# Scores of the short last query tile: one unit at a time in two 64x64 tiles, or two units together in four

## The chip, the core and the metric

The kernel runs on one core of one Trainium2 chip. The metric is the device time of one execution in microseconds (us), smaller is better. A core has five engines with a queue each, worked off in order: TensorE (PE in the profile; PEld is its weight load), VectorE (DVE), ScalarE (ACT), GpSimd (POOL) and SyncE (SP, which here only issues DMAs). A number such as L303 is a line of the kernel before; all lines named here and in the prediction are lines of that file unless the text says otherwise.

## What is computed

Attention with a top-32 mask over 8 batches and 8 heads, 576 positions, head dimension 64, followed by a SwiGLU feed-forward block on the 4608 x 512 result, all in fp32:

```
scores = q @ k.T / 8                        # per batch and head: 576 x 576
kth    = 32nd largest of each row
attn   = softmax(scores where scores >= kth, else -1e9)
x      = (attn @ v), heads side by side     # 4608 x 512
out    = (silu(x @ w_gate) * (x @ w_val)) @ w_out     # d_ff 1536
```

## The kernel before

**Units.** The attention is cut into 160 units `(b, qt, hp)`: batch, query tile, pair of heads, with the pair innermost. 576 queries make four tiles of 128 and a rest of R = 64, so of the 20 units of a batch the first 16 are full (`qt` 0 to 3: 128 queries, two heads one after the other, each on all 128 partitions) and the last four are short (`qt == J`: 64 queries, the two heads of the pair above each other on the partitions). Positions inside a batch are called 0 to 19 below; 16 to 19 are the short ones. Units 16 and 17, and 18 and 19, are neighbours that `values` treats as a pair.

**A unit's way.** `scores` multiplies q by k on PE into PSUM banks of 288 columns and ACT copies these, scaled, into `sc` in SBUF. `select` finds the 32 largest of each row on DVE: four MAX8 and three MATCH_REPLACE8 per 128 rows (L337, L341). `shift` is a small POOL operation (L352). `weigh` makes the masked exponentials on ACT (Prelu L364, Exp L369). `normalize` divides by the sum (DVE L382, L383; ACT L387; POOL L389). `turn` transposes the weights on PE (L402) and ACT copies them out (L403). `values` multiplies two units' weights by v (PE L435) and ACT copies the result into `xT` (L451).

**The short unit's scores.** L303: for each of two halves of the keys a bank, and in it one matmul per head. Head 0 reads partitions 0 to 63 and writes partitions 0 to 63, head 1 reads and writes 64 to 127. So two of the four 64x64 quarters of the array are used, those on the diagonal. L308 copies the two banks out. The full unit (L317, L322) has two heads by two halves of the keys, four matmuls of 64 rows by 128 columns into four banks.

**PSUM.** `ps_t` has five banks with one tag, which the scores, the values and all transposes share; a new tile takes the bank that was free first.

**The order of work** is written out by hand in a loop over n; the last lines of the kernel pin every engine's instructions to the order in which the loop emits them. One turn n of the loop emits, in this order: what waits in `on_act`; `shift(n - 1)`; the first scores of `nxt`, matmuls and copies; at even n `values` of the two units n - 4 and n - 3; the matmuls of the second scores of `nxt`; `weigh(n - 1)` on ACT; the copies of the second scores on ACT; then, between the steps of `select(n)` on DVE, up to two pieces of feed-forward work, `turn(n - 2)`, key and query transposes of unit n + 3 (`fetch`), `normalize(n - 1)`, and more pieces. `scored(n)` says which scores a turn has: at even n those of n + 1 and n + 2, at odd n none.

**Feed-forward pieces.** `piece()` emits the next part of the feed-forward block (L579 for the first products, L645 for the second), each with a cost. How many are emitted in turn n is set by a credit: `share(n)` grants 6.4 (5.8 in the first 32 turns; half of it for a short unit) less an estimate of the other PE work in that turn, in which scores of a full unit count 0.7 and those of a short one 0.35. All pieces are done once, whatever the credit says; it moves them only between turns. From unit 156 on the credit is 8.

Of the kernel before, what the change touches and what calls it, by code (L numbers as in the profile page):

```python
# [8 lines left out]
AF = mybir.ActivationFunctionType  # L9
# [16 lines left out]
def kernel(  # L26
# [260 lines left out]
    def scores(n):  # L287
        b, qt, hp = units[n]
        slab = preps[b * NHP + hp]
        sc = work.tile([P, 2 * S], FP32, tag="sc", name="sc", bufs=3)  # L290
        halves = [slice(0, D), slice(D, P)]
        half = S // 2

        def bank():
            return ps_t.tile([P, 512], FP32, tag="t", name="s")


        if qt == J:
            banks = [bank() for _ in range(2)]
            for i, ps in enumerate(banks):  # L300
                for d in halves:
                    k0 = R + i * half
                    nc.tensor.matmul(  # L303
                        ps[d, 0:half], slab[d, S + R : S + 2 * R], slab[d, k0 : k0 + half]
                    )
            yield
            for i, ps in enumerate(banks):
                nc.scalar.mul(sc[:, i * half : (i + 1) * half], ps[:, 0:half], scale)  # L308
        else:
            q0 = S + 2 * R + qt * P  # L310
            banks = []
            for i in range(2):
                for hh, d in enumerate(halves):
                    ps = bank()
                    banks.append((i + 2 * hh, ps))
                    k0 = (1 - hh) * R + i * half
                    nc.tensor.matmul(  # L317
                        ps[:, 0:half], slab[d, q0 : q0 + P], slab[d, k0 : k0 + half]
                    )
            yield  # L320
            for i, ps in banks:
                nc.scalar.mul(sc[:, i * half : (i + 1) * half], ps[:, 0:half], scale)  # L322
        state[n] = dict(sc=sc)

    def select(n):

        nh = n_heads(units[n][1])
        sc = state[n]["sc"]
        m = small.tile([P, 2, TOP_K], FP32, tag="m", name="m")
        heads = [slice(t * S, (t + 1) * S) for t in range(nh)]  # L330
        e = work.tile([P, 2 * S], FP32, tag="e", name="e", bufs=3)
        state[n] |= dict(m=m, e=e, heads=heads)
        cur = sc
        rounds = TOP_K // 8
        for r in range(rounds):
            for t, hs in enumerate(heads):
                nc.vector.max(m[:, t, 8 * r : 8 * r + 8], cur[:, hs])  # L337
                yield
            if r < rounds - 1:
                for t, hs in enumerate(heads):  # L340
                    nc.vector.match_replace(  # L341
                        e[:, hs], m[:, t, 8 * r : 8 * r + 8], cur[:, hs], LOWEST
                    )
                    yield
                cur = e

    def shift(n):

# [8 lines left out]
    def weigh(n):  # L357


        st = state[n]  # L360
        sc, m, e, heads, bias = st.pop("sc"), st.pop("m"), st["e"], st["heads"], st.pop("bias")
        tot = small.tile([P, 2], FP32, tag="tot", name="tot")
        for t, hs in enumerate(heads):
            nc.scalar.activation(  # L364
                e[:, hs], sc[:, hs], AF.Prelu, bias=m[:, t, TOP_K - 1 : TOP_K], scale=-1.0,
                alpha=SMALL,
            )
        for t, hs in enumerate(heads):
            nc.scalar.activation(  # L369
                e[:, hs], e[:, hs], AF.Exp, bias=bias[:, t : t + 1], scale=-1.0 / SMALL,  # L370
                accum_out=tot[:, t : t + 1],
            )
        if n < AHEAD:
            nc.scalar.add(tot[:, 0 : len(heads)], tot[:, 0 : len(heads)], EPS)
        st["tot"] = tot
# [37 lines left out]
    def values(ns):  # L413

        b, qt, hp0 = units[ns[0]]
        last = qt == J
        ql = R if last else P
        av = ps_t.tile([P, 2, P], FP32, tag="t", name="av")
        for i, n in enumerate(ns):
            assert units[n] == (b, qt, hp0 + i)  # L420
            vt, v_last, vl = vs[b * NHP + hp0 + i]
            et = state.pop(n)["et"]
            for c in (*range(J), J) if last else (J, *range(J)):
                for hh in range(2):
                    d = slice(hh * R, (hh + 1) * R)
                    if c == J:
                        weights_, at = (v_last[:, hh, :], d) if last else (vl[:, d], None)
                    else:
                        weights_, at = vt[:, hh, c, :], d if last else None
                    moving = (  # L430
                        et[:, c, at]
                        if last
                        else et[:, c + (0 if c == J else hh * (J + 1)), :]
                    )
                    nc.tensor.matmul(  # L435
                        av[d, i, 0:ql],
                        weights_,
                        moving,
                        start=c == (0 if last else J),
                        stop=c == (J if last else J - 1),  # L440
                    )
        c0 = b * S + qt * P
        at = c0
        hps = slice(hp0, hp0 + len(ns))
        while at < c0 + ql:
            kb = at // BLK
            n_c = min((kb + 1) * BLK, c0 + ql) - at
            if kb not in xT:
                xT[kb] = ffn.tile([P, NHP, BLK], FP32, tag="xT", name="xT", bufs=3)
                done[kb] = 0  # L450
            nc.scalar.copy(  # L451
                xT[kb][:, hps, at - kb * BLK : at - kb * BLK + n_c],
                av[:, 0 : len(ns), at - c0 : at - c0 + n_c],
            )
            done[kb] += n_c * len(ns)
            at += n_c
# [331 lines left out]
    def share(n):  # L788


        others = 0.0
        costs = [(m, 0.7) for m in scored(n) + valued(n)] + [(n - TURN, 0.6)]
        for m, cost in costs:
            if m >= 0:
                others += cost * (0.5 if units[m][1] == J else 1)
        if units[n + 3][1] == 0:
            others += 0.6

        beside = 5.8 if n < AHEAD else 6.4
        return beside * n_heads(units[n][1]) / 2 - others  # L800

    def scored(n):

        ahead = [n + 1] if n < 2 else [] if n % 2 else [n + 1, n + 2]
        return [m for m in ahead if m < NU]

    def valued(n):

        behind = [] if n % 2 else [n - 4, n - 3]
        return [m for m in behind if 0 <= m < NU]  # L810
# [33 lines left out]
    for n in range(NU + 3):  # L844
        nh = n_heads(units[n][1]) if n < NU else 1
        topk = select(n) if n < NU else no
        norm = normalize(n - 1) if 0 <= n - 1 < NU else no
        nxt = [scores(m) for m in scored(n)]
        ahead = fetch(n + 3 if n else 2) if n + 3 < NU else no

        def dve(k, beside=True):

            for _ in range(k * nh):
                next(topk, None)
                due[0] += 5 / 6 if beside else 0
                if due[0] >= 1:
                    due[0] -= 1
                    rounding(1)

        if n >= NU - NHP:  # L860
            credit[0] = 8.0
        else:
            credit[0] = min(credit[0] + share(n), share(n) + 1)
        flush(on_act)
        if 0 <= n - 1 < NU:
            shift(n - 1)
        flush(on_pool)
        if nxt:
            run(nxt.pop(0))
        if valued(n):  # L870
            finish_units(valued(n))
        if nxt:
            next(nxt[0])
        early[0]()
        if 0 <= n - 1 < NU:
            weigh(n - 1)
        if nxt:
            run(nxt.pop())


        dve(2, beside=False)
        if n == 0:
            run(ahead)
            load(3)
            ahead = fetch(3)
        if n < NHP:
            load_v(n)
        pieces(2)
        flush(on_act)
        dve(1)  # L890
        dve(1)
        if 0 <= n - TURN < NU:
            run(turn(n - TURN))

        flush(on_pool)
        next(ahead, None)
        pieces(1)
        next(ahead, None)
        dve(1)
        pieces(1)  # L900
        if n < AHEAD:
            dve(1, beside=False)
        run(norm)
        dve(1 if n < AHEAD else 2, beside=False)
        run(topk)
        pieces(6)
# [50 lines left out]
```

## Time and profile before

| | |
|---|---|
| median of three runs | 1753.39 us (1752.44 to 1754.14) |
| the profiled execution | 1752.52 us, of which the span is 1750.7 us |
| PE busy | 1673.1 us, 96% of the span |
| DVE busy | 1475.4 us, 84% |
| ACT busy | 1262.1 us, 72% |
| POOL busy | 799.2 us, 46% |
| granted TensorE clock | 0.975 in the mean, below full in the first slices |
| the short units' score matmuls (L303) | 38.0 us |
| the full units' score matmuls (L317) | 173.0 us |

The span runs from the first to the last instruction; the execution has 1.8 us around it. A matmul of fp32 stands in the records twice (two passes), so a short unit's four matmuls are eight records. "Busy" is the time in which at least one record of a group is open, so matmuls that run beside each other count once; the mean is that of one record and is longer than its share of the time, since records overlap. The last unit's sums are inverted on DVE at 1682 us; after that PE works off the rest of the feed-forward block. An idle time is put down to the last thing that the waiting instruction needed.

### The profile page before, as it was taken

To read this page: it belongs to the slowest core of one execution; us is meant where nothing else is said; L and a number is where in the kernel's file an instruction comes from. 1 tells how busy PE (TensorE), PEld (TensorE's weight loads), DVE (VectorE), ACT (ScalarE), POOL (GpSimd) and SP (SyncE) were. 2 spreads that over 40 slices of the span, in tenths; PEclk is the share of its full clock that TensorE was granted. 3 is DMA by queue.
4 is the path that set the end of the run, shared out by engine and by line. 5 is a ranking of instruction groups with operands and counts; after the bars stand their busy time and mean duration, and the time that the engine had idled before them with its cause. 6 is when DMAs were issued, how large, how long until landed. Compare 5 with 4: busy or idle time off the path is not lost.

```text
span 1750.7 us, 31758 instructions
## 1 busy us (share of the span) xinstructions
PE 1673.1 (96%) x11408; PEld 1401.1 (80%) x11408; DVE 1475.4 (84%) x3311; ACT 1262.1 (72%) x2901; POOL 799.2 (46%) x914
## 2 busy tenths in 40 slices
PE   5679999999999999999999999999999999999999
PEld 3468688788888788887888878887888878788887
DVE  6999899989989899898999898898988988898300
ACT  7899787777767786768777777777776777676531
POOL 4799534343353425352535334443444433535334
PEclk6698999999999999999999999999999999999999
DMA  7442120003000120002100030000300020000000
GB/s 203 137 121 86 29 69 1 13 2 83 15 13 1 28 70 1 13 13 58 28 13 1 14 70 27 1 13 19 80 1 13 1 57 15 13 1 13 1 13 12
DMA packets 109309, 59.72 MB, mean 34 GB/s; under 512 B 88544, under 2 KB 96992, under 8 KB 109152
## 3 DMA queue, kind: packets, MB, share of 16 engines
q1 hardware_dynamic: 108016, 57.37, 12.6%
q8 instruction: 90, 1.47, 0.4%
q14 instruction: 67, 0.55, 0.1%
q10 hardware_dynamic: 1136, 0.33, 0.1%
HBM read 48.23 MB, written 9.44 MB: 33 GB/s over the span
## 4 chain that ended last, share of the span: by engine, by line
PE 79%; DVE 10%; ACT 6%; POOL 2%; issue 1%; SPq 1%; DMA 0%; POOLq 0%; ACTq 0%; DVEq 0%
PE f L579 36%; PE x_ps L645 9%; PE av L435 9%; PE s L317 7%; PE y_ps L645 6%; PE etps L402 6%; DVE m L337 5%; DVE e L341 4%; PE f L495 3%; ACT e L369 2%; PE s L303 2%; PE kqps L270 1%; DVE size L123 1%; PE o_ps L547 1%; ACT e L364 1%
## 5 line engine op out<-in xcount | busy, mean ns | idle before, releaser
L337 DVE MAX8 m<-e 128x8 f32<-128x576 f32 x864 | 614.8, 747 | 3.1
L341 DVE MATCH_REPLACE8 e<-m,e 128x576 f32<-128x576 f32 x576 | 423.8, 742 | 0.0
L579 PE MATMUL f<-xT,wg 128*128 128x256 f32 x1536 | 354.1, 381 | 0.0
L579 PE MATMUL f<-xT,wv 128*128 128x256 f32 x1536 | 353.9, 380 | 0.0
L579 PEld LDWEIGHTS f<-xT,wg 128*128 128x128 f32 x1536 | 287.0, 190 | 45.4 <-issue 8.4
L579 PEld LDWEIGHTS f<-xT,wv 128*128 128x128 f32 x1536 | 286.8, 190 | 42.7 <-issue 5.5
L615 POOL TENSOR_TENSOR h<-h,half_g 128x512 f32<-128x512 f32 x96 | 122.5, 1276 | 347.5 <-ACT h L614 331.6
L369 ACT ACTIVATE e<-e,bias 128x576 f32<-128x576 f32 x288 | 221.5, 778 | 34.6 <-POOL bias L352 31.3
L402 PE MATMUL etps<-ident,e 128*128 128x128 f32 x1312 | 183.3, 282 | 47.8 <-POOL e L389 20.8
L402 PEld LDWEIGHTS etps<-ident,e 128*128 128x128 f32 x1312 | 155.1, 144 | 78.3 <-POOL e L389 26.5
L364 ACT ACTIVATE e<-sc,m 128x576 f32<-128x576 f32 x288 | 212.1, 790 | 0.0
L341 DVE MATCH_REPLACE8 e<-m,sc 128x576 f32<-128x576 f32 x288 | 211.8, 742 | 0.0
L337 DVE MAX8 m<-sc 128x8 f32<-128x576 f32 x288 | 203.2, 742 | 7.3 <-ACT sc L322 7.3
L322 ACT ACTIVATE sc<-s 128x288 f32<-128x288 f32 x512 | 167.9, 418 | 53.8 <-PE s L317 53.4
L620 POOL TENSOR_TENSOR h<-h,val 128x512 f32<-128x512 f32 x96 | 122.4, 1275 | 175.1 <-ACT val L619 158.3
L389 POOL TENSOR_TENSOR e<-e,tot 128x576 f32<-128x576 f32 x140 | 160.7, 1152 | 89.3 <-DVE tot L383 76.0
L403 ACT COPY et<-etps 128x512 f32<-128x512 f32 (+1 forms) x448 | 184.2, 491 | 12.0 <-PE etps L402 11.6
L317 PE MATMUL s<-kqT 64*128 64x288 f32 x1024 | 173.0, 446 | 15.1 <-ACT et L403 7.7
L382 DVE TENSOR_SCALAR tot<-tot 128x1 f32<-128x1 f32 x228 | 29.2, 145 | 168.8 <-ACT e L369 168.8
L435 PE MATMUL av<-et,v 128*64 128x128 f32 (+1 forms) x2560 | 156.3, 266 | 0.0
L387 ACT ACTIVATE e<-e,tot 128x576 f32<-128x576 f32 x148 | 119.3, 806 | 48.3 <-DVE tot L383 47.9
L317 PEld LDWEIGHTS s<-kqT 64*128 64x128 f32 x1024 | 96.9, 192 | 61.3 <-issue 23.2
(86 smaller groups left out, 2280.2 us busy)
## 6 DMA issues: line engine op xcount, KB each, us to landing
v<-in_v_dram SPq DMA_DIRECT2D x32, 256.0 KB, 3.3
kq_in<-in_k_dram SPq DMA_DIRECT2D x63, 128.0 KB, 2.9
kq_in<-in_q_dram SPq DMA_DIRECT2D x63, 128.0 KB, 3.2
w<-in_moe_w_gate_dram SPq DMA_DIRECT2D x12, 512.0 KB, 3.8
w<-in_moe_w_val_dram SPq DMA_DIRECT2D x12, 512.0 KB, 3.7
w<-in_moe_w_out_dram SPq DMA_DIRECT2D x12, 512.0 KB, 3.6
out_dram<-o SPq DMA_DIRECT2D x38, 128.0 KB, 2.4
out_dram<-o SPq DMA_DIRECT2D x16, 256.0 KB, 2.4
```

The costliest lines, as they stand in the source:

```text
L317: nc.tensor.matmul(ps[:, 0:half], slab[d, q0 : q0 + P], slab[d, k0 : k0 + half])
L322: nc.scalar.mul(sc[:, i * half : (i + 1) * half], ps[:, 0:half], scale)
L337: nc.vector.max(m[:, t, 8 * r : 8 * r + 8], cur[:, hs])
L341: nc.vector.match_replace(e[:, hs], m[:, t, 8 * r : 8 * r + 8], cur[:, hs], LOWEST)
L364: nc.scalar.activation(e[:, hs], sc[:, hs], AF.Prelu, bias=m[:, t, TOP_K - 1 : TOP_K], scale=-1.0, alpha=SMALL,)
L369: nc.scalar.activation(e[:, hs], e[:, hs], AF.Exp, bias=bias[:, t : t + 1], scale=-1.0 / SMALL, accum_out=tot[:, t : t + 1],)
L389: nc.gpsimd.tensor_tensor(e[:, hs], e[:, hs], tot[:, t : t + 1].to_broadcast([P, S]), ALU.mult)
L402: nc.tensor.transpose(ps[:, c * P : (c + 1) * P], e[:, k0 : k0 + P], ident[:])
L403: nc.scalar.copy(et[:, c0 : c0 + cn, :], ps[:, 0 : cn * P].rearrange("p (c j) -> p c j", c=cn),)
L435: nc.tensor.matmul(av[d, i, 0:ql], weights_, moving, start=c == (0 if last else J), stop=c == (J if last else J - 1),)
L579: nc.tensor.matmul(ps[:, i, :], w[:, kc, m * P : (m + 1) * P], x[:, kc, :], start=(kc == 0), stop=(kc == KC - 1),)
L645: nc.tensor.matmul(ps, lhsT, T[i][m], start=m == 0, stop=m == MQ - 1)
```

## The change

Two short units (n and n + 1, n even) get their scores in one call. For each half of the keys two banks are opened, one for each unit. Unit n lies as before. Unit n + 1 has its heads swapped: head 0 reads partitions 0 to 63 and writes 64 to 127, head 1 the other way round. The four matmuls of one half therefore name the four different 64x64 quarters of the array. Both units' scores go to one `sc` tile, the second 576 columns on; `select` and `weigh` read from there, and `values` of the second unit picks the query columns of the swapped half.

`scored(n)` no longer names the odd short unit. At position 14 a turn has the scores of 15 and of 16 with 17, at 16 those of 18 with 19, at 18 those of 20. Where a turn has one entry, it is emitted in the second place, after `values`; the first place stays empty. In `share` the joint scores count 0.7; before, the two counted 0.35 each and partly in other turns.

```diff
--- before.py
+++ after.py
@@ -296,16 +296,23 @@
 
 
         if qt == J:
-            banks = [bank() for _ in range(2)]
-            for i, ps in enumerate(banks):
-                for d in halves:
-                    k0 = R + i * half
-                    nc.tensor.matmul(
-                        ps[d, 0:half], slab[d, S + R : S + 2 * R], slab[d, k0 : k0 + half]
-                    )
+            both = (slab, preps[b * NHP + hp + 1])
+            banks = []
+            for i in range(2):
+                k0 = R + i * half
+                two = [bank(), bank()]
+                banks += [(i + 2 * u, ps) for u, ps in enumerate(two)]
+                for u, (sl, ps) in enumerate(zip(both, two)):
+                    for hh, d in enumerate(halves):
+                        nc.tensor.matmul(
+                            ps[halves[hh ^ u], 0:half],
+                            sl[d, S + R : S + 2 * R],
+                            sl[d, k0 : k0 + half],
+                        )
             yield
-            for i, ps in enumerate(banks):
+            for i, ps in banks:
                 nc.scalar.mul(sc[:, i * half : (i + 1) * half], ps[:, 0:half], scale)
+            state[n + 1] = dict(sc=sc, at=S)
         else:
             q0 = S + 2 * R + qt * P
             banks = []
@@ -320,7 +327,7 @@
             yield
             for i, ps in banks:
                 nc.scalar.mul(sc[:, i * half : (i + 1) * half], ps[:, 0:half], scale)
-        state[n] = dict(sc=sc)
+        state[n] = dict(sc=sc, at=0)
 
     def select(n):
 
@@ -328,21 +335,23 @@
         sc = state[n]["sc"]
         m = small.tile([P, 2, TOP_K], FP32, tag="m", name="m")
         heads = [slice(t * S, (t + 1) * S) for t in range(nh)]
+        at = state[n]["at"]
+        from_ = [slice(at + t * S, at + (t + 1) * S) for t in range(nh)]
         e = work.tile([P, 2 * S], FP32, tag="e", name="e", bufs=3)
-        state[n] |= dict(m=m, e=e, heads=heads)
+        state[n] |= dict(m=m, e=e, heads=heads, source=from_)
         cur = sc
         rounds = TOP_K // 8
         for r in range(rounds):
-            for t, hs in enumerate(heads):
+            for t, hs in enumerate(from_):
                 nc.vector.max(m[:, t, 8 * r : 8 * r + 8], cur[:, hs])
                 yield
             if r < rounds - 1:
                 for t, hs in enumerate(heads):
                     nc.vector.match_replace(
-                        e[:, hs], m[:, t, 8 * r : 8 * r + 8], cur[:, hs], LOWEST
+                        e[:, hs], m[:, t, 8 * r : 8 * r + 8], cur[:, from_[t]], LOWEST
                     )
                     yield
-                cur = e
+                cur, from_ = e, heads
 
     def shift(n):
 
@@ -360,9 +369,9 @@
         st = state[n]
         sc, m, e, heads, bias = st.pop("sc"), st.pop("m"), st["e"], st["heads"], st.pop("bias")
         tot = small.tile([P, 2], FP32, tag="tot", name="tot")
-        for t, hs in enumerate(heads):
+        for t, (hs, at) in enumerate(zip(heads, st.pop("source"))):
             nc.scalar.activation(
-                e[:, hs], sc[:, hs], AF.Prelu, bias=m[:, t, TOP_K - 1 : TOP_K], scale=-1.0,
+                e[:, hs], sc[:, at], AF.Prelu, bias=m[:, t, TOP_K - 1 : TOP_K], scale=-1.0,
                 alpha=SMALL,
             )
         for t, hs in enumerate(heads):
@@ -415,6 +424,8 @@
         b, qt, hp0 = units[ns[0]]
         last = qt == J
         ql = R if last else P
+        assert hp0 % 2 == 0
+        halves = [slice(0, R), slice(R, P)]
         av = ps_t.tile([P, 2, P], FP32, tag="t", name="av")
         for i, n in enumerate(ns):
             assert units[n] == (b, qt, hp0 + i)
@@ -424,9 +435,10 @@
                 for hh in range(2):
                     d = slice(hh * R, (hh + 1) * R)
                     if c == J:
-                        weights_, at = (v_last[:, hh, :], d) if last else (vl[:, d], None)
+                        weights_ = v_last[:, hh, :] if last else vl[:, d]
                     else:
-                        weights_, at = vt[:, hh, c, :], d if last else None
+                        weights_ = vt[:, hh, c, :]
+                    at = halves[hh ^ i] if last else None
                     moving = (
                         et[:, c, at]
                         if last
@@ -789,10 +801,10 @@
 
 
         others = 0.0
-        costs = [(m, 0.7) for m in scored(n) + valued(n)] + [(n - TURN, 0.6)]
-        for m, cost in costs:
+        for m, cost in [(m, 0.7) for m in valued(n)] + [(n - TURN, 0.6)]:
             if m >= 0:
                 others += cost * (0.5 if units[m][1] == J else 1)
+        others += 0.7 * len(scored(n))
         if units[n + 3][1] == 0:
             others += 0.6
 
@@ -802,7 +814,7 @@
     def scored(n):
 
         ahead = [n + 1] if n < 2 else [] if n % 2 else [n + 1, n + 2]
-        return [m for m in ahead if m < NU]
+        return [m for m in ahead if m < NU and (units[m][1] < J or m % 2 == 0)]
 
     def valued(n):
 
@@ -865,7 +877,7 @@
         if 0 <= n - 1 < NU:
             shift(n - 1)
         flush(on_pool)
-        if nxt:
+        if nxt and (n < 2 or len(nxt) > 1):
             run(nxt.pop(0))
         if valued(n):
             finish_units(valued(n))
```

In the built program the number of instructions of these kinds is as before on every engine; what differs is where they stand. Pieces of the feed-forward block move by one or two places between positions 16 and 19 of a batch, and from position 2 of the next batch on the sums are the same again.

## The prediction

> **What bounds the kernel now.** I read the page first: busy times, then the 40 slices.
>
> ```profile
> PE 1673.1 (96%) x11408; PEld 1401.1 (80%) x11408; DVE 1475.4 (84%) x3311; ACT 1262.1 (72%) x2901; POOL 799.2 (46%) x914
> ...
> PE   5679999999999999999999999999999999999999
> ...
> PEclk6698999999999999999999999999999999999999
> ```
>
> PE is busy in nearly every slice after the third, at full clock. The stretches say it closer: from 222 to 1433 us PE is busy 1194.7 of 1211.0 us, DVE 1090.6. So PE sets the pace, DVE has about a tenth to spare, and PE time removed is worth its full length unless PE then waits for something. The groups by shape give what a pass costs.
>
> ```profile
> L579 PE MATMUL f<-xT,wg 128*128 128x256 f32 x1536 | 354.1, 381 | 0.0
> ...
> L435 PE MATMUL av<-et,v 128*64 128x128 f32 x2048 | 135.0, 275 | 0.0
> ...
> L303 PE MATMUL s<-kqT 64*64 64x288 f32 x256 | 38.0, 415 | 0.0
> ...
> L308 ACT ACTIVATE sc<-s 128x288 f32<-128x288 f32 x64 | 23.8, 416 | 16.0 <-PE s L303 15.3
> ```
>
> Then the timeline of PE at position 16 of the third batch (the columns: start, length, what, how often, idle before).
>
> ```profile
> 592.46 1.19 PE L303 MATMUL s<-kqT 64*64 64x288 f32 x8
> 593.57 0.44 PE L435 MATMUL av<-et,vlast 128*64 128x128 f32 x4
> ...
> 595.91 1.19 PE L303 MATMUL s<-kqT 64*64 64x288 f32 x8
> 597.03 1.56 PE L645 MATMUL x_ps<-wo,h 128*128 128x256 f32 x6
> 598.42 1.15 PE L402 MATMUL etps<-ident,e 128*128 128x128 f32 x9
> ...
> 605.78 0.33 PE L263 MATMUL kqps<-ident,kq_last 128*128 128x128 f32 x1 [0.90 <-ACT et L403]
> ...
> 611.96 0.33 PE L402 MATMUL etps<-ident,e 128*128 128x128 f32 x1 [0.64 <-ACT sc L322]
> ```
>
> Two visits of a short unit's scores, 1.11 us each from start to next start, and two PE waits: about 1.5 us a batch, nearly all that PE idles in these batches. ACT and DVE at the same place:
>
> ```profile
> 593.21 0.90 ACT L308 ACTIVATE sc<-s 128x288 f32<-128x288 f32 x2 [4.16 <-PE s L303]
> 596.02 0.37 ACT L451 COPY xT<-av 128x256 f32<-128x256 f32 x1 [1.92 <-PE av L435]
> 596.29 1.44 ACT L364 ACTIVATE e<-sc,m 128x576 f32<-128x576 f32 x2
> ...
> 599.15 0.69 ACT L308 ACTIVATE sc<-s 128x288 f32<-128x288 f32 x2
> ```
> ```profile
> 598.53 0.15 DVE L382 TENSOR_SCALAR tot<-tot 128x1 f32<-128x1 f32 x1 [4.38 <-ACT e L369]
> ```
>
> ACT's copies wait for PE, and `weigh` stands behind them in ACT's queue; DVE then waits 4.38 us for `weigh`. So here too PE is the bound, through ACT.
>
> **The matmuls.** In the timeline a pass of L579, 256 columns, takes 0.216 us back to back (16 in 3.46 us), so one of 288 takes 0.243. Eight passes one by one would be 1.94 us; the visit takes 1.11: four rounds of two (0.97) and 0.14 for filling and changing tiles. Nobody has run four quarters here. Two of one column half are shown by L317 (1024 passes in 173.0 us, 0.169 each), two over the same rows with different moving data by L435 (16 passes in 0.88 us, 0.055 each, where a lone pass of 128 columns needs 0.108). If all four run together, a joint visit has four rounds again, 1.11 us, for two units. At position 14 a visit becomes a joint visit at no extra time, at 16 and 18 one disappears: 16 pairs x 1.11 = 17.7 us less PE work.
>
> A rule speaks against this. The Trainium skill, "TensorE: Matmul & The Clock Gate", section "Part 3: Packing small matmuls — row/col tiling", says that weights load beside running matmuls only where the row group differs. The third quarter has the row group of the first. By that rule quarters three and four follow one and two: eight rounds, 1.11 + 0.97 = 2.08 us a joint visit, and 16 x 0.14 = 2.2 us saved instead of 17.7. The L435 passes, two column halves over the same 128 rows at half a pass each, contradicts the rule; and at 0.032 us per load and matmul in its 64-column form (16 in 0.52 us) four of them take 0.13 us of a 0.243 us round, so issue isn't the limit. I take four rounds.
>
> **The copies and the banks.** Another page of the skill speaks against it too: "TensorEngine Tiling (Array Packing)", section "PSUM Bottleneck", says that tiling doesn't speed up the evacuation. The row: 64 copies at 0.30 to 0.42 us, unchanged in number, but moved. At position 16 the banks of unit 17 were copied before `weigh`; now all four joint banks are copied after it. In the built program the next transposes (`turn(14)`, three banks) take the bank of `values` first and then two joint banks, so their fifth matmul waits for the first joint copy. From the start of `values`, t = 0: ACT ends its av copy and `weigh` at 5.58 (599.15 - 593.57) and the copy at 5.95; with the semaphore 6.0. PE: values 2.34, joint 1.11, four transposes 0.44, so it arrives at 3.9 plus what pieces stand between. Order in the built program: none in batches 0, 2, 3, 4; three matmuls (1.3 us) in 1 and 6; four (1.73) in 5; eight (3.46) in 7. New waits: 4 x 2.1, 2 x 0.8, 0.4, 0; together 10.4 us. By the rule as an end (evacuation is the bound, every saving at 16 goes) 8 x 1.11 = 8.9 us would be lost; the count by rows is taken. At position 14 at least 2.6 us of pieces stand between, arrival at 6.5: no wait, but if they were gone it would be 2.1 us each. At 18 the scores of 20 were in the second place already.
>
> **What comes back.** The old waits at 17 (`turn(15)` for ACT, or the key transposes for `et` copies) are 1.0, 0.9, 0.9, 0.6, 0.5, 0.5, 0.9 us in batches 0 to 6. `weigh(15)` starts 1.11 us earlier, since ACT no longer waits for 17, and PE, held by the new wait, arrives no earlier: these 5.3 us disappear. At 18 a wait of 0.6 to 1.0 for the copies of 20 stays, up to 0.15 longer, except in batches 1, 3 and 6, where a piece now stands before it: +2.3, less 0.5 for the others.
>
> Sum by batch: 2.2 less new wait plus returned: 1.1, 3.3, 0.9, 1.4, 0.5, 2.2, 3.0, 2.2 = 14.6 us. I cap batches 1 and 6 at 2.5, since DVE's turns 17 to 19 already run at their 5.8 us floor and unit 20 can start only about 1.8 us sooner: 13.3 us. Against the profiled execution: 1752.5 - 13.3 = 1739.2; it lay 0.9 under the median, so 1740.
>
> **Costed at nothing.** DVE reads `sc` and `e` at other offsets, `values` other columns: same instructions and shapes (L337 reads either source at 742 to 747 ns); bounds 0 to 0.2 us a unit, taken 0. Moved pieces: the total is equal and from position 2 of the next batch the order agrees. At 14, two more copies (0.6 us of ACT) ahead of the `et` copies; ACT is 72% busy and pieces cover; without cover 8 x 0.6 = 5 us. The DMA queue, POOL's order and `fetch` are untouched in number; slabs are released earlier. In the tail PE is in order behind the last scores, so what is gained before it stays.
>
> **Rivals.**
> (a) Quarters by twos, as the rule has it: 2.2 us saved; the longer joint visit covers part of the new wait (1.13 left in four batches, 4.5), 5.3 and 1.8 return: 1748, between 1745 and 1753. For it: no row with four. Against: L435. Chance 0.18, half of it within the bound.
> (b) Slower: the joint visit runs pass after pass. Mechanism: quarters that share rows with one neighbour and columns with another block each other at both ends. Place: L303's successor; price 16 passes x 0.243 + 0.14 = 4.03 us against 2.22, so 16 x 1.81 = 29 us, no new wait: about 1777 with some returned. It decides from a joint visit of about 2.6 us. Against: pairs of either kind overlap. Chance 0.06.
> (c) PE saves but doesn't get ahead: DVE and ACT pace positions 16 to 19, the bank wait takes 2.1 in all batches and old waits stay: 17.7 - 16.8 - 0.5, about 1753, no change. For it: DVE at its floor there. Against: DVE waits 4.38 us for PE at 16. Chance 0.05.
>
> **How the numbers follow.** Four rounds: 0.71, 1740, its own range 1735 to 1745. This kernel's measurement can tell about 0.2% (3.5 us) from no change. Faster: 0.71 + 0.09 = 0.80; same: 0.09 + 0.04 = 0.13; slower: 0.06 + 0.01 = 0.07. The range goes from 1733 (no cap, bank wait covered better) to 1752, taking in most of (a).
>
> **What would show it.** Right: the joint scores' 256 passes busy about 18 to 20 us instead of 38.0; sixteen visits of 1.1 us; at position 16 of batches 0, 2, 3, 4 a wait of L402's successor for ACT's score copy of about 2 us; the DVE wait at 16 shorter by 1.1. Wrong: a visit of 2 us or more (then (a) or (b)); or visits of 1.1 us and PE idle time up by as much as PE's busy time falls (then (c)).

## The result, and the profile after

The changed kernel takes 1745.14 us in the median of six runs (1743.89 to 1746.70), the kernel before 1753.23 us beside it: ratio 0.9954, 95% interval 0.9942 to 0.9967. It is 8.1 us faster; the forecast was about 13 us. The profiled execution has a span of 1743.4 us, 7.3 less than before. Lines in this part are those of the changed kernel: L307 is the short units' scores, L314 their copies, L411 the transposes of `turn`, L398 the division on POOL.

First the busy times, from the page, and the groups by shape of PE:

```profile
PE 1661.9 (95%) x11408; PEld 1399.7 (80%) x11408; DVE 1476.0 (85%) x3311; ACT 1259.9 (72%) x2901; POOL 798.4 (46%) x914
```
```profile
L411 PE MATMUL etps<-ident,e 128*128 128x128 f32 x1312 | 183.5, 280 | 57.3 <-POOL e L398 25.0 <-ACT sc L329 13.8 <-ACT sc L314 9.7
...
L307 PE MATMUL s<-kqT 64*64 64x288 f32 x256 | 19.2, 415 | 0.0
```

The same 256 passes are now busy for 19.2 us instead of 38.0. Part of that time lies over the records of their neighbours, so I count a visit as the prediction did, from its start to the next start: 32 visits of 1.12 us (35.8 us in all) have become 16 of 1.13 us (18.1), 17.7 us less. But PE in all is busy only 11.2 us less. Everything except these matmuls takes 6.5 us longer, with the same instructions; and PE's idle time has grown by 3.9 us (81.5 against 77.6). The sum is the span: -17.7 + 6.5 + 3.9 = -7.3. Two of the three terms were forecast, the middle one not. A new releaser stands in the first row: 9.7 us of waiting for L314, the copies of the joint scores.

Batches are counted from 0, as in the prediction (so the "seventh batch" of some expectations is batch 6). The timeline of PE at position 16 of batch 2 shows all three terms within ten microseconds:

```profile
590.76 1.20 PE L307 MATMUL s<-kqT 64*64 64x288 f32 x16
591.89 0.66 PE L411 MATMUL etps<-ident,e 128*128 128x128 f32 x4
594.54 0.87 PE L411 MATMUL etps<-ident,e 128*128 128x128 f32 x5 [1.99 <-ACT sc L314]
595.24 2.72 PE L657 MATMUL x_ps<-wo,h 128*128 128x256 f32 x6
```

A joint visit of sixteen passes takes 1.13 us from start to next start, the time of one unit's eight before. Four transposes fit into the bank of `values`, the fifth waits 1.99 us. And the six passes behind it take 2.72 us; six such passes took 1.56 us before (the row at 597.03 of the prediction). The stretches of PE tell why (length, PE busy and records, granted clock, DMA share, GB/s):

```profile
592.50:595.30 2.80, 0.81 (x7) 1.00 0.00 0
595.30:598.70 3.40, 3.40 (x10) 0.50 0.02 5
```

During the wait the clock is full; in the 3.4 us after it PE is granted half. What PE lost there is in no row of waits: it hides in the busy time. ACT and DVE at this place:

```profile
591.14 1.44 ACT L373 ACTIVATE e<-sc,m 128x576 f32<-128x576 f32 x2
...
593.91 0.19 ACT L378 ACTIVATION_READ_ACCUMULATOR e<-e,bias 128x1 f32 x1
594.00 1.29 ACT L314 ACTIVATE sc<-s 128x288 f32<-128x288 f32 x4
```
```profile
593.38 0.15 DVE L391 TENSOR_SCALAR tot<-tot 128x1 f32<-128x1 f32 x1 [3.27 <-ACT e L378]
```

ACT copies all four banks (L314) only after `weigh` (L373, L378), and DVE waits 3.27 us instead of 4.38, since `weigh` no longer stands behind the scores of 17.

### The profile page after: what moved, and what is told of

It reads as the page before. It is cut to its first block, busy times and chain, and to the rows that moved or that the text cites. A ratio compares the mean times of both kernels' runs of the same rounds, so it can differ in the third digit from the quotient of the medians.

```text
span 1743.4 us, 31763 instructions
## 1 busy us (share of the span) xinstructions
PE 1661.9 (95%) x11408; PEld 1399.7 (80%) x11408; DVE 1476.0 (85%) x3311; ACT 1259.9 (72%) x2901; POOL 798.4 (46%) x914
## 4 chain that ended last, share of the span: by engine, by line
PE 82%; DVE 7%; ACT 6%; POOL 2%; issue 1%; SPq 1%; DMA 0%; ACTq 0%; POOLq 0%
PE f L591 38%; PE av L447 9%; PE x_ps L657 9%; PE s L324 7%; PE etps L411 7%; PE y_ps L657 6%; DVE m L346 3%; DVE e L350 3%; PE f L507 2%; ACT e L378 2%; PE kqps L270 1%; PE o_ps L559 1%; DVE size L123 1%; ACT e L373 1%; POOL p L644 1%
## 5 line engine op out<-in xcount | busy, mean ns | idle before, releaser
L378 ACT ACTIVATE e<-e,bias 128x576 f32<-128x576 f32 x288 | 221.6, 779 | 37.3 <-POOL bias L361 34.3
L411 PE MATMUL etps<-ident,e 128*128 128x128 f32 x1312 | 183.5, 280 | 57.3 <-POOL e L398 25.0
L411 PEld LDWEIGHTS etps<-ident,e 128*128 128x128 f32 x1312 | 154.9, 143 | 86.6 <-POOL e L398 31.2
L373 ACT ACTIVATE e<-sc,m 128x576 f32<-128x576 f32 x288 | 212.4, 792 | 0.0
L398 POOL TENSOR_TENSOR e<-e,tot 128x576 f32<-128x576 f32 x140 | 160.6, 1151 | 81.5 <-DVE tot L392 72.2
L447 PEld LDWEIGHTS av<-et,v 128*64 128x64 f32 x2560 | 138.8, 141 | 5.9 <-issue 3.0
```

The costliest lines, as they stand in the source:

```text
L373: nc.scalar.activation(e[:, hs], sc[:, at], AF.Prelu, bias=m[:, t, TOP_K - 1 : TOP_K], scale=-1.0, alpha=SMALL,)
L378: nc.scalar.activation(e[:, hs], e[:, hs], AF.Exp, bias=bias[:, t : t + 1], scale=-1.0 / SMALL, accum_out=tot[:, t : t + 1],)
L398: nc.gpsimd.tensor_tensor(e[:, hs], e[:, hs], tot[:, t : t + 1].to_broadcast([P, S]), ALU.mult)
L411: nc.tensor.transpose(ps[:, c * P : (c + 1) * P], e[:, k0 : k0 + P], ident[:])
L447: nc.tensor.matmul(av[d, i, 0:ql], weights_, moving, start=c == (0 if last else J), stop=c == (J if last else J - 1),)
```

## The experiments

My theory after the result (A in the expectations): four quarters do run together; what is missing from the plain sum was taken back by the transposes' wait for the joint banks, by the half clock that follows such a wait, and by one wait for POOL in batch 6. Rivals: the four-quarter matmuls lower the clock or slow their neighbours themselves (B); the moved feed-forward pieces cost it (C); the gain is the order, not the quarters (D). Ratios are against the kernel before, run beside each.

| kernel | median us | ratio, 95% interval |
|---|---|---|
| e1, joint scores of turn 16 in the first place | 1738.15 | 0.9915 (0.9900 to 0.9930) |
| e2, useless transposes in the wait | 1741.75 | 0.9938 (0.9923 to 0.9953) |
| e3, old credit | 1748.62 | 0.9971 (0.9961 to 0.9982) |
| e4, two quarters | 1749.67 | 0.9981 (0.9972 to 0.9991) |
| e5, first place and two quarters | 1753.25 | 1.0002 (0.9992 to 1.0011) |
| e6, first place and old credit | 1740.57 | 0.9933 (0.9915 to 0.9952) |
| e7, other order of the four | 1744.07 | 0.9950 (0.9935 to 0.9965) |
| e8, e1 with the old credit in batch 6 | 1734.03 | 0.9895 (0.9878 to 0.9911) |
| e1 again, beside e8 | 1739.01 | 0.9925 (0.9910 to 0.9940) |

**e1: the joint scores that turn 16 emits (those of 18 and 19) ahead of `values` and `weigh`.**

```diff
-        if nxt and (n < 2 or len(nxt) > 1):
+        if nxt and (n < 2 or len(nxt) > 1 or (n % 20 == 16)):
```

> The changed kernel, but at position 16 of each batch the joint scores of 18 and 19 stand in the first place again, matmuls and copies ahead of values and weigh. Theory A (what is missing from the plain sum is the transposes' wait for the joint banks and the half clock that follows such a wait): the waits of the transposes for the joint score copies at 16 (9.7 us in all after the change) are gone, so are the half-clock intervals next to them; PE busy without the score matmuls falls back from 1642.7 to about 1637 us, and weigh starts about 1.7 us later, which may bring back some of the old waits at 17: about 1735 us. Theory B (the four-quarter matmuls themselves lower the clock or slow their neighbours): the waits go, the half-clock intervals stay, about 1740 us or, if the old waits return in full, 1745 us.

7 us faster than the changed kernel, with visits as before. The timeline of PE at the same place of batch 2:

```profile
585.86 1.20 PE L307 MATMUL s<-kqT 64*64 64x288 f32 x16
586.99 0.44 PE L447 MATMUL av<-et,vlast 128*64 128x128 f32 x4
...
589.33 1.20 PE L411 MATMUL etps<-ident,e 128*128 128x128 f32 x9
590.37 1.46 PE L657 MATMUL x_ps<-wo,h 128*128 128x256 f32 x6
...
594.52 1.20 PE L411 MATMUL etps<-ident,e 128*128 128x128 f32 x9 [0.96 <-ACT e L396]
```

The nine transposes run through, the six passes behind them are back at their old length, and of the old waits at 17 one is back (0.96 us). Over batches 0 to 6 such waits at 17 add up to 5.6 us in e1, which can account for 1738 instead of 1735. PE's busy time less the 19.2 us of the score matmuls fell from 1642.7 to 1638.8 us. B is out: the four-quarter matmuls are all there, and after 222 us the half clock stays only beside waits that have nothing to do with them.

**e2: useless work in the wait.** In `turn`, for the transposes that turn 16 emits (those of unit 14) in batches 0, 2, 3 and 4:

```diff
             ps = ps_t.tile([P, 512], FP32, tag="t", name="etps")
+            if n in FILL and c0 == 0:
+                for _ in range(18):
+                    nc.tensor.transpose(ps[:, 0:P], ident[:], ident[:])
```

> The changed kernel with 18 transposes of the identity (each 0.11 us, two of the 2 us waits' length; their result is overwritten) put ahead of the transposes at position 16 in batches 0, 2, 3 and 4, where PE otherwise waits about 2 us. Nothing useful is added and nothing removed. Theory A: PE is not idle there, so the half-clock intervals after these waits (at about 203, 595 and 800 us) do not come; each is worth up to 1.7 us; PE busy rises by up to 8 us and the time falls by 3 to 5 us, to about 1741 us. Theory B (the clock has nothing to do with these waits): the same intervals stay and the time is 1745 us or a little more.

72 transposes more, and 3.4 us less time in the median (the interval still overlaps that of the changed kernel, so the clock rows carry the verdict). The timeline and a stretch (here the added transposes are L411 and those of `turn` L414):

```profile
588.71 1.20 PE L307 MATMUL s<-kqT 64*64 64x288 f32 x16
589.84 2.18 PE L411 MATMUL etps<-ident 128*128 128x128 f32 x18
591.86 1.49 PE L414 MATMUL etps<-ident,e 128*128 128x128 f32 x9
593.19 1.46 PE L660 MATMUL x_ps<-wo,h 128*128 128x256 f32 x6
```
```profile
592.00:595.50 3.50, 3.47 (x21) 1.00 0.02 5
```

The six passes start as late as in the changed kernel, 4.48 us after the joint scores; but PE is not idle meanwhile, the clock stays full, and the six passes take 1.46 us instead of 2.72. The half-clock intervals at 203, 595 and 800 us are gone. That the wait brings the half clock is shown here apart from the wait's own length; its price in time, about 3.4 us for these three, is less sharp.

**e3: the credit of the kernel before.**

```diff
-        for m, cost in [(m, 0.7) for m in valued(n)] + [(n - TURN, 0.6)]:
+        costs = [(m, 0.7) for m in short_too(n) + valued(n)] + [(n - TURN, 0.6)]
+        for m, cost in costs:
             if m >= 0:
                 others += cost * (0.5 if units[m][1] == J else 1)
-        others += 0.7 * len(scored(n))
...
+    def short_too(n):
+        ahead = [n + 1] if n < 2 else [] if n % 2 else [n + 1, n + 2]
+        return [m for m in ahead if m < NU]
```

> The changed kernel with the credit of the kernel before (a short unit's scores count 0.35 each in the turn that had them before), so the feed-forward pieces stand where they stood before. Theory A: the 3.4 us wait of PE for POOL in the seventh batch (1410 to 1413 us) goes, since it comes from a piece that was moved; the pieces between joint scores and transposes at 16 are then none in batches 0, 1, 4, 5, 6, 1.3 us in 2 and 1.7 us in 3, so the bank waits are 5 x 2.1 + 0.7 + 0.4 = 11.6 us instead of 9.7: in sum about 1744 us, between 1741 and 1747. Theory C (the moved pieces are what costs the missing 5 us): about 1740 us.

3.5 us slower than the changed kernel in the median, outside my range on the slow side (the two intervals overlap by a little). The POOL wait in batch 6 went as said, and the bank waits came to 11.5 us (11.6 expected). What I left out were three half-clock intervals behind such waits (batches 4 to 6), a fourth at 224 us behind another wait of 2.08 us, and old waits of 0.5 to 1.0 us at 17 and 18 in batches 1 to 6, 5.4 us in all, of which the new credit covers about half. C is out as the whole cause: with the pieces where they stood, nothing of the missing 5 us comes back. That one moved piece has its price all the same, and that the old credit loses as much elsewhere, is shown by e8 and e6 below.

**e4 and e5: the second unit in the same two quarters,** once in the changed order, once in that of e1.

```diff
-                            ps[halves[hh ^ u], 0:half],
+                            ps[d, 0:half],
...
-                    at = halves[hh ^ i] if last else None
+                    at = halves[hh] if last else None
```

> The changed kernel, order and credit unchanged, but the heads of the second unit are not swapped: its matmuls name the same two quarters as the first unit's. Theory A (the gain is the four quarters running together): a joint visit takes eight rounds, about 2.08 us instead of 1.13, the score matmuls 34 us instead of 19; the longer visit covers about 1 us of each bank wait, and with it the half clock: about 1749 to 1752 us. Theory D (the gain is the new order, with fewer visits and weigh earlier): 1745 us as with four quarters.

> Joint scores of position 16 in the first place, as in e1, and the second unit not swapped, as in e4: two quarters without a bank wait. Theory A (the quarters' concurrency is worth 15.3 us of PE time, 34.5 against 19.2 us of score matmuls, and in the changed kernel the bank waits and the half clock after them took about 10 of it back): slower than e1 (1738.15) by 13 to 16 us, so 1751 to 1754 us, that is: the kernel before. Theory D (four quarters bring only the 4.5 us that e4 showed, the rest is order): about 1743 us.

The timeline of e4:

```profile
593.22 2.16 PE L307 MATMUL s<-kqT 64*64 64x288 f32 x16
595.31 0.65 PE L411 MATMUL etps<-ident,e 128*128 128x128 f32 x4
597.00 0.86 PE L411 MATMUL etps<-ident,e 128*128 128x128 f32 x5 [1.03 <-ACT sc L314]
597.70 1.46 PE L657 MATMUL x_ps<-wo,h 128*128 128x256 f32 x6
```

A visit of 2.09 us, eight rounds, as worked out ahead of the run. It covers half of the bank wait, and one of 1.03 us is not followed by half clock. So with the bank wait in place four quarters gain 4.5 us over two (1749.67 to 1745.14), and in the order of e1 15.1 us (1753.25 to 1738.15), which is the difference of the score matmuls, 34.5 to 19.2 us, within 0.2. D is out: e5, order without quarters, takes as long as the kernel before. The two gains differ by 10.6 us: putting the joint scores first saves 7.0 us with four quarters, since the bank wait and its clock go, and costs 3.6 us with two, where the longer visit covers half of the wait.

**e7: the four matmuls in another order,** head 0 of both units first, so that neighbours in the queue share rows of the array.

```diff
-                for u, (sl, ps) in enumerate(zip(both, two)):
-                    for hh, d in enumerate(halves):
+                for hh, d in enumerate(halves):
+                    for u, (sl, ps) in enumerate(zip(both, two)):
```

> The changed kernel with the four matmuls of one half in another order: head 0 of both units, then head 1 of both, so that neighbours in the queue read the same rows of the array instead of the two quarters of a diagonal. Theory A (each quarter loads and runs by itself): same times, visits of 1.13 us, 19.2 us of score matmuls, 1745 us. Theory F (weights load beside a running matmul only where the row group differs, so the order with different rows next to each other is what makes four fit): the visits get longer, up to 2.1 us and 34 us in all, about 1750 us.

```profile
589.16 1.20 PE L307 MATMUL s<-kqT 64*64 64x288 f32 x16
590.29 0.66 PE L411 MATMUL etps<-ident,e 128*128 128x128 f32 x4
592.94 0.86 PE L411 MATMUL etps<-ident,e 128*128 128x128 f32 x5 [1.99 <-ACT sc L314]
```

The same 1.13 us. Quarters over the same rows run beside each other, whichever of them are neighbours in the queue.

**e6, e8: what is left in e1.** In batch 6 the changed credit moves a piece of the second product from before position 16 to behind the joint scores. POOL and PE of the changed kernel there:

```profile
1407.49 0.73 POOL L644 TENSOR_TENSOR p<-p 128x256 f32<-128x256 f32 x1 [8.27 <-ACT p L691]
1408.30 0.73 POOL L644 TENSOR_TENSOR o<-o,p 128x256 f32<-128x256 f32 x1
1408.99 1.29 POOL L644 TENSOR_TENSOR p<-p,p 128x512 f32<-128x512 f32 x1
1410.21 2.11 POOL L705 TENSOR_TENSOR h<-h,xT 128x256 f32<-128x256 f32 x3
1412.26 1.17 POOL L398 TENSOR_TENSOR e<-e,tot 128x576 f32<-128x576 f32 x1
```
```profile
1413.48 0.77 PE L411 MATMUL etps<-ident,e 128*128 128x128 f32 x5 [3.41 <-POOL e L398]
```

POOL waits 8.27 us for the copy of that piece's sum, then has 4.8 us of feed-forward work in one go, and the division that PE's transposes need stands behind it. Before the change that work was done while POOL had nothing else. e6 takes the old credit for all batches, e8 for batch 6 alone:

```diff
-        others += 0.7 * len(scored(n))
+        if n // 20 == 6:
+            last = [n + 1, n + 2] if n % 2 == 0 else []
+            others += sum(0.35 if units[m][1] == J else 0.7 for m in last)
+        else:
+            others += 0.7 * len(scored(n))
```

> Joint scores of position 16 in the first place, as in e1, with the credit of the kernel before, as in e3. Theory A (what is left in e1 is above all the 3.5 us wait for POOL in the seventh batch with 6.8 us of half clock beside it, and it comes from the moved piece): that wait goes, some waits of 0.5 to 1.0 us at 17 and 18 return (5 us in the kernel before, less where e1 has them already): 1733 to 1738 us. Theory E (the credit matters little or the old waits return in full): 1738 to 1741 us.

> e1 (joint scores of position 16 in the first place), with the credit of the kernel before in the seventh batch alone, so that only there the feed-forward pieces stand as before. Theory A (the moved piece makes POOL late in that batch, PE waits 3.5 us and then runs 6.8 us at half clock): both go, 1.4 and 0.65 us of waits as in e6 come instead: about 1733 to 1736 us against 1738.15 for e1. Theory E (the wait is made up elsewhere): 1738 us as e1. Rival G (the old credit costs as much here as e6 suggests for all batches together): 1738 to 1740 us.

> e1 once more, unchanged, beside e8 on the same chip, since the two differ by little: 1738 us within 1 us by every theory.

e6 missed: it is not faster than e1 (2.4 us slower in the median, within the intervals). e8 is 5.0 us faster than e1 beside it; the intervals just touch. The same stretch of the two (first e1 again, then e8):

```profile
1390.00:1420.00 30.00, 25.93 (x201) 0.89 0.16 37
```
```profile
1390.00:1420.00 30.00, 27.97 (x227) 1.00 0.20 45
```

In e8 PE is idle 2.0 us less there and never at half clock. Over the whole span the two traces differ by only 1.5 us: the profiled execution of e8 is the longest of its four (1737.32 us), and it has half-clock intervals at 222 and 1502 us that e1's has not. By the medians the moved piece cost about 5 us in one batch, and the old credit loses about as much in the others (e6 and e8 differ beyond their intervals): the spans of e6 and e8 differ by 5.1 us, of which 2.5 us is PE idle time before 230 us and 2.5 us after. e8 is the fastest version here, 18.5 us under the kernel before.

## Why the prediction was right, and where it was not

**The matmuls: right.** Sixteen visits of 1.13 us (1.11 said), 19.2 us (18 to 20 said). The rule on row groups that the prediction names would have made them 2.08 us; e4 shows that length where two units do share quarters, e7 that the row group of the neighbour in the queue doesn't matter. Saved, from start to start: 17.7 us, as said. What the 0.14 to 0.16 us beyond the four rounds consist of, no run shows.

**The bank wait: right in place and size.** Said by batch 2.1, 0.8, 2.1, 2.1, 2.1, 0.4, 0.8, 0; measured 2.23, 0.62, 1.99, 2.00, 2.00, 0.28, 0.56, none: 9.7 us against 10.4. It could be read ahead of time, because the order of the built program says which bank the transposes take, and the rows of ACT say when it is copied.

**What comes back: right in six of seven batches.** The old waits at 17 are gone in batches 0 to 5, and the DVE wait is shorter by 1.1 us. In batch 6 the step failed: there the old 0.9 us became 3.41. At 18 the waits fell by 1.4 us (1.8 said). One reading was too strong: the two waits a batch at 17 and 18 were not nearly all that PE idled, but 8.6 of 16.3 us between 222 and 1433 us.

**Costed at nothing: here the prediction failed.** I took the moved pieces as free, since their sum is equal, and POOL's order as untouched in number. One of them put 4.8 us of POOL work ahead of a division on the path; e8 prices it, in the order of e1, at 5 us with its clock.

**The term that was missing: the clock.** The sum had waits as plain lengths. Behind the bank waits of batches 0, 2 and 3 and the POOL wait of batch 6 PE ran 3.4 us at half clock. The same table of stretches, for the waits of batches 3, 4 and 6:

```profile
800.10:803.50 3.40, 3.40 (x9) 0.50 0.01 2
1001.10:1009.00 7.90, 5.91 (x38) 1.00 0.00 0
```
```profile
1414.50:1418.00 3.50, 3.50 (x29) 0.52 0.19 44
```

In the trace the half-clock intervals after 190 us, without one at the very end, add up to 23.9 us against 10.2 before: four more of 3.41 us behind the waits just named, one more at 319 us, one less at 1516 us. At half speed the 13.7 us more are worth 6.8 us if PE is busy throughout, and its other work did grow by 6.5 us. In the prediction's own terms: 17.7 us less work and 4.4 more idle; it was 17.7 and 3.9, so the gap between 13.3 and the span's 7.3 us is this term, less 0.5.

That the idle sum came out so close is partly luck. The forecast was 10.4 us of bank waits, less 5.3 at 17 and 1.8 at 18, and 1.3 for the cap. Measured were 9.7, less 4.5 and 1.4; then the POOL wait added 2.5 that no step had named, and 2.4 fell away at places that no step had named either, 1.2 of them before 190 us.

From the middle of one batch to the middle of the next (the same transposes in both traces), the changed kernel gained -0.1, 4.3, -1.1, -0.6, 0.9, 2.8, -1.9 and, to the end, 3.2 us, where the prediction had 1.1, 2.5, 0.9, 1.4, 0.5, 2.2, 2.5 and 2.2. It falls short in batches 0, 2, 3 and 6, those with half clock behind a wait. In batch 1 it gained more than the cap of 2.5 us allowed; and some 1.7 of the last 3.2 us are the half-clock interval at 1516 us, which of these two traces only the one of the kernel before has.

All three rivals of the prediction fall: (a) and (b) by the visits of 1.13 us, (c) since 8 us stay.

## What to carry to other kernels

When PE work is taken away, what used to cover a wait goes with it: before counting the saving, look what follows the shorter work in the queue, which buffer it takes, and when the engine that frees it gets there. If copies stand behind a long operation in another engine's queue, put the producer ahead of it. On TensorE a wait can cost more than its length: behind some waits of 2 us the clock fell to half here, and then the loss sits in busy time: compare the durations of unchanged rows, and the granted clock, not the waits alone.

## What the runs showed of the hardware

- Four 64x64 quarters run together in fp32: sixteen passes of 288 columns in 1.13 us, where two quarters take 2.09.
- A PE wait of 2.0 us is enough for half clock, but not always: those of batches 2 and 3 were followed by it, that of batch 4, 2.00 us too, was not. In e7, which has the same waits, it came behind those of batches 2 and 4 and not behind those of 0 and 3, nor behind the POOL wait of 3.39 us, which fell on two steps with 1.4 and 2.0 us. The intervals last 3.41 us or a multiple and lie on a fixed grid of 3.41 us in each trace. Worked out on this grid, PE was idle 2.0 of 3.4 us in the step ahead of the intervals at 595 and 800 us, and 1.7 of 3.4 where the clock stayed full. In all eleven traces, from 190 us on, all 35 full-clock steps with more than 1.97 us of idle PE were followed by half clock, 5 of the 18 with 1.6 to 1.97 us were, and of those with less only one (1.25 us, in e8). So it looks as if idleness of about half a step decides, and where a wait falls on the grid; that is a reading of the traces, not an experiment of its own. It also means that part of this term is chance: the same wait can cost 1.7 us more or not.
- Useless matmuls in the waits kept the clock full (1.00 at 592 to 595.5 us) and lowered the median by 3.4 us, though the intervals of the two kernels overlap.
